# The values' product of two chunks at once over all 128 partitions, with zeros between their values

## The chip, the core and the metric

The kernel runs on one core of one Trainium2 chip. The metric is the device time of one execution in microseconds (us); less is better. Engines are named as in the profile: PE is TensorE's matmul, PEld its weight load, DVE VectorE, ACT ScalarE, POOL GpSimd, SP SyncE, which issues all transfers here.

## What is computed

Attention over local windows, then two matrix products with a gate between them. All inputs are f32.

```python
# q, k, v: [4, 8, 768, 64]; mem_k, mem_v: [4, 8, 8, 64]; w_in: [512, 2048]; w_out: [2048, 512]
for c in range(24):                                   # chunks of 32 queries
    l, r = max(0, c*32 - 16), min(768, c*32 + 32 + 8)
    k_full = concat([mem_k, k[:, :, l:r]], axis=2)    # 64 keys at most
    v_full = concat([mem_v, v[:, :, l:r]], axis=2)
    s = (1/8) * q[:, :, c*32:c*32+32] @ k_full^T
    a = exp(s - max(s)); a = a / (sum(a) + 1e-9)
    out[:, :, c*32:c*32+32] = a @ v_full
x = out as [3072 tokens, 512]
h = x @ w_in
g = where(h >= 1, h, where(h <= -1, 0, (h + 1)**2 / 4))
result = g @ w_out
```

## The kernel before, in words

The 3072 tokens are worked on in six blocks of 512 (`NB`, `TB`), each in two halves of 256 tokens, which are eight chunks of 32 queries; a chunk sees `W` = 64 keys. Eight heads are four pairs (`NP`). The two large products (`pe_hidden`, `pe_out`) run with x, gate and weights split into a rounded f32 part and a remainder (`F32R`), three terms each; the small products of the attention are plain f32 (`F32`).

The first three blocks' attention, the decoding of the weights and the first two blocks' large products are written in one hand-made order (`FIRST`, line 32; `g` is the attention of the first block in four parts, `n0` to `n3` that of the halves of the second and third block, `L` a transfer from the list `loads`, line 613, `w` and `u` a decoding). After it, a loop over (block, slice of 128 hidden columns) runs the large products of blocks three to six, and puts the attention of the next block's two halves between them (line 659): scores at slice 3 or 9 of the block, then one stage a slice: softmax, transposes, values, split. `InOrder` (line 61) keeps every engine's work in the order in which the program writes it.

A half of block three and later goes like this. `pe_scores` puts queries on the partitions of PSUM. DVE takes off the maximum, ACT the exponential, DVE divides; `transpose_prob` turns the probabilities on DVE in 32 x 32 squares, so that the 64 keys of one chunk come to lie in partitions 0 to 63 and those of another in 64 to 127 (`a` in the code counts these two). `pe_rows` (line 398) then multiplies: weights are 64 keys x 32 queries, the moving operand is 64 keys x 64 values, and the two chunks of a pair are two matmuls on the two halves of the array's rows. `rows_out` (line 416) copies the result by ACT from two PSUM banks, one for each `a`; `turn_rows` turns it on DVE, `split_high` and `split_low` make x.

`load_v` (line 133) brings the values of a half by one transfer into a tile of 8 KB a partition, a single buffer that is free once the product before has read it. The first block (`first_attention`, line 225) uses weights of 128 keys (two heads) and 64 columns, with the probabilities in a tile `pt_apart` (line 222) that GpSimd clears at the start; both the first and the second block write x^T directly. `load_first_qk` and `load_w` (lines 109 and 141) bring first q and k and the first two weight tiles in two transfers each, each of them a half of every row of its array in memory.

Of the kernel before, what the change touches and what calls it, by code (L numbers as in the profile page):

```python
# [8 lines left out]
F32 = mybir.dt.float32  # L9
F32R = mybir.dt.float32r  # L10
BF16 = mybir.dt.bfloat16
U32 = mybir.dt.uint32
# [4 lines left out]
P = 128  # L17
CHUNK, LEFT, RIGHT = 32, 16, 8
# [39 lines left out]
SLICED = (0,1)  # L58
# [13 lines left out]


@with_exitstack
def attn_ffn_kernel(ctx: ExitStack, tc: tile.TileContext, first_qk, first_v, qk, vw, w, out):
    nc = tc.nc
    engines = (nc.tensor, nc.scalar, nc.vector, nc.gpsimd, nc.sync)
    pe, act, dve, pool, sp = (InOrder(tc, e) for e in engines)
    NP = first_qk.shape[0]
    NM = 8  # L80
    D = P // 2
    W = NM + LEFT + CHUNK + RIGHT
    DM = NP * P
    NPW = w.shape[0]
    NFC = NPW
    NB = qk.shape[0] + 1
    SEQ = 24
# [1 line left out]
    n2 = 2 * DM  # L89
# [3 lines left out]
    apool = ctx.enter_context(tc.tile_pool(name="apool", bufs=1))  # L93
# [6 lines left out]
    def two_banks(tag, name):  # L100
        return ps_2.tile([P, 2, 512], F32, name=name, tag=tag)
# [3 lines left out]
    QKN = HT + HT // CHUNK * W  # L105
    VN = HT // CHUNK * W
    qk_of, v_of = {}, {}

    def load_first_qk(g, r):

        if (0, g) not in qk_of:
            if g < 2:
                t = apool.tile([P, 2, 2 * QKN], F32, name="qk0", tag="qk")
                qk_of[0, 0], qk_of[0, 1] = t[:, 0], t[:, 1]
            else:
                qk_of[0, g] = const.tile([P, 2 * QKN], F32, name=f"qk0_{g}", tag=f"w_{NPW - 5 + g}")
        at = slice(r * QKN, (r + 1) * QKN)
        sp.dma_start(qk_of[0, g][:, at], first_qk[g, :, at])

    def load_first_v(g):  # L120
        if (0, g) not in v_of:
            if g < 2:
                t = apool.tile([P, 2, 2 * VN], F32, name="v0", tag="v")
            else:
                t = const.tile([P, 2, 2 * VN], F32, name="v0_2", tag=f"w_{NPW - 1}")
            v_of[0, g - g % 2], v_of[0, g - g % 2 + 1] = t[:, 0], t[:, 1]
        sp.dma_start(v_of[0, g], first_v[g])
# [3 lines left out]
        sp.dma_start(t, qk[blk - 1, half].rearrange("p (h f) -> p h f", h=NP))  # L131

    def load_v(blk, half):
        t = v_of[blk, half] = apool.tile([P, NP, VN], F32, name="v", tag="v")
        sp.dma_start(t, vw[blk - 1, half].rearrange("p (h f) -> p h f", h=NP))


    place = {key: divmod(n, 2) for n, key in enumerate(weight_order(NFC))}
    ws, raw = {}, {}

    def load_w(i, parts=(0, 1)):
        if i not in raw:
            tag = f"w_{NPW - 6 - i}" if i < len(SLICED) else f"w_{i}"
            raw[i] = const.tile([P, 2 * n2], U32, name=f"w_{i}", tag=tag)
        a, b = parts[0] * n2, (parts[-1] + 1) * n2
        sp.dma_start(raw[i][:, a:b], w[i, :, a // 2 : b // 2].bitcast(U32))

    def weights(which, fc, part):
        i, j = place[which, fc]
# [27 lines left out]
    scores_of, prob, prob_t, banks, rows_of, turned, xts, both = {}, {}, {}, {}, {}, {}, {}, {}  # L177
    first = 2
# [40 lines left out]
    NG = 2 * 2 * 2  # L219
    PLACES = (("s", "s"), ("a0", "a0"), ("a1", "a1"), ("a1", "s"))  # L220

    pt_apart = apool.tile([P, 2, NG // 2, 2, P], F32, name="pt0", tag="pt")
    pool.memset(pt_apart, 0.0)

    def first_attention(g):
        half, u = divmod(g, 2)
        c0 = half * NCH // 2
        src = qk_of[0, g].rearrange("p (r n) -> p r n", r=2)
# [17 lines left out]
            mask(c0 + c, s[j * CHUNK : (j + 1) * CHUNK, :, :, t])  # L246
        if u == 0:
            both[half, "pr"] = apool.tile([P, 2, NG, W], F32, name="pr0", tag="pr")
        pr, pt = both[half, "pr"][:, u], pt_apart[:, u]
        n = 2 * 2  # L250
        mx = apool.tile([P, NG], F32, name="mx", bufs=2)
        m4 = mx.rearrange("p (h r t) -> p h r t", h=2, r=2)
# [143 lines left out]
            yield  # L396
        banks.pop(key)

    def pe_rows(key, outs):

        banks[key] = outs
        pt = prob_t.pop(key).rearrange("p b (h r t) q -> p b h r t q", h=2, r=NP)
        v = v_of.pop(key).rearrange("p r (t b h d) -> p r t b h d", t=2, b=2, h=2)
        for r in range(NP):
            for t in range(2):
                for b in range(2):
                    for a in range(2):
                        rows = slice(a * D, (a + 1) * D)
                        for h in range(2):
                            to, c0 = (2 * h + b) * CHUNK, (r * 2 + t) * D  # L410
                            pe.matmul(
                                outs[a][to : to + CHUNK, c0 : c0 + D],
                                pt[rows, b, h, r, t],
                                v[rows, r, t, b, h],
                                start=True,
                                stop=True,
                            )

    def rows_out(key):

        xr = rows_of[key] = apool.tile([P, NP, 2, 2, D], F32, name="xr", tag="pt")
        for a, src in enumerate(banks.pop(key)):
            act.copy(xr[:, :, :, a], src.rearrange("p (r t d) -> p r t d", r=NP, t=2))

    def x_half(x, half):
        return x[:, :, half * HT : (half + 1) * HT]
# [23 lines left out]
    def attention(key):  # L450

        pe_scores(key)
        yield
        yield from less_max(key)
        act.activation(prob[key], prob[key], AF.Exp, scale=SCALE)
        yield
        yield from normalise(prob[key])
        yield from transpose_prob(key)
        if key[0] < first:
            pe_values(key)  # L460
            yield
            x_high(key)
            yield
            yield from x_low(key)
            return
        ps = two_banks("s", "ps_x")
        pe_rows(key, [ps[:, a] for a in range(2)])
        yield
        rows_out(key)
        yield  # L470
        yield from turn_rows(key)
        split_high(key)
        yield
        yield from split_low(key)
# [131 lines left out]
    def keep_warm(n):  # L606
# [5 lines left out]

    loads = [
        (load_first_qk, 0, 0), (load_first_qk, 0, 1), (load_first_qk, 1, 0), (load_first_qk, 1, 1),
        (load_first_v, 0), (load_w, 0, (0,)), (load_w, 0, (1,)), (load_first_v, 1),
        (load_first_qk, 2, 0), (load_first_qk, 2, 1), (load_w, 1, (0,)), (load_w, 1, (1,)),
        (load_first_qk, 3, 0), (load_first_qk, 3, 1), (load_first_v, 2), (load_first_v, 3),
    ]
    loads += [(load_w, i) for i in range(2, NPW)]
# [39 lines left out]
    for s in range(first * NFC, steps):  # L659
# [3 lines left out]
            if after(k_scores)[0] < NB:  # L663
                load_qk(*after(k_scores))
        if k_values is not None:
            ps = two_banks("s", "ps_x")
            pe_rows(k_values, [ps[:, a] for a in range(2)])
            if after(k_values)[0] < NB:
                load_v(*after(k_values))
        if s > first * NFC:  # L670
# [48 lines left out]
def _lay_out(q, k, v, mem_k, mem_v, moe_w_in, moe_w_out):  # L719
# [16 lines left out]
    def transposed(a):  # L736
# [7 lines left out]
    k0 = kw.transpose(0, 4, 7, 3, 1, 2, 5, 6).reshape(NB * 2, 2 * D, NP, NCH // 2 * W)  # L744
    kw = _np.stack([kw[:, :, 0], kw[:, :, 1][..., ::-1, :, :]], axis=2)
    kw = kw.transpose(0, 4, 7, 3, 1, 2, 5, 6).reshape(NB * 2, 2 * D, NP, NCH // 2 * W)
    qk0 = _np.concatenate([qt, k0], axis=3)[0:2].reshape(2, 2 * D, 2, -1).transpose(0, 2, 1, 3)
    qk = _np.concatenate([qt, kw], axis=3).reshape(NB, 2, 2 * D, -1)[1:]
    vw = windows(mem_v, v).reshape(NB, NT, 4, NP, 2, W, D)

# [5 lines left out]
    n = DF // 128  # L756
# [3 lines left out]
        moe_w_out.reshape(n, 128, DM),  # L760
    )
    w = _np.stack([slices[which][fc] for which, fc in weight_order(n)])
    w = w.reshape(n, 2, 128, DM).transpose(0, 2, 1, 3).reshape(n, 128, 2 * DM)
    arrays = {

        "first_qk": qk0.reshape(NP, 2 * D, -1),
        "first_v": v0.reshape(NP, 2 * W, NCH * D),
        "qk": qk,
        "vw": v1.reshape(NB - 1, 2, 2 * W, -1),
        "w": _np.ascontiguousarray(w).view(_np.int64),  # L770
    }
    return {name: _np.ascontiguousarray(a) for name, a in arrays.items()}
# [23 lines left out]
```

## Time and profile before

| | |
|---|---|
| time, median of 3 runs | 591.45 us (591.18 to 591.91) |
| the profiled execution | 591.77 us, its span 590.0 us |
| granted clock of TensorE, mean | 0.999 |
| busy share of the span | PE 97%, PEld 81%, DVE 57%, ACT 44% |
| chain that ended last | PE 94%, ACT 2%, DMA 2%, DVE 1% |
| matmul records | 5364 |
| moved by DMA | 55.30 MB, 94 GB/s over the span |

The page gives, for one profiled execution, each engine's busy time, the chain of work that ended last, and groups of instructions. A line of a group reads: engine, operation, what is written <- what is read, rows * columns of the weights, partitions x columns of the moving operand, count | busy us, mean ns | idle time of the engine just before them. A plain f32 matmul leaves two records and two weight loads; one on rounded f32 leaves one. All program lines read L69, because one helper issues every operation; tiles tell the groups apart. Ends of matmuls are modelled, so spans from start to start say more than their durations.

### The profile page before, as it was taken

How to read it: one execution, taken by the hardware profiler on the slowest of the kernel's cores; microseconds unless marked ns; L12 is line 12 of the kernel's file. 1: busy time of each engine (PE TensorE's matmuls, PEld its weight loads, DVE VectorE, ACT ScalarE, POOL GpSimd, SP SyncE). 2: the span in 40 equal slices, each digit the busy share in tenths (PEclk: the TensorE clock that was granted, in tenths of full speed). 3: DMA queues.
4: the chain of work that ended last, by engine and by line, in shares of the span. 5: the costliest groups of instructions: out<-in, count | busy, mean ns of one | idle time of the engine just before them, and what ended most of it. 6: DMA issues, size and time to landing. Idle time of an engine off the chain costs nothing.

```text
span 590.0 us, 12019 instructions
## 1 busy us (share of the span) xinstructions
PE 575.1 (97%) x5364; PEld 476.4 (81%) x5364; DVE 338.0 (57%) x497; ACT 257.2 (44%) x430; POOL 2.4 (0%) x7
## 2 busy tenths in 40 slices
PE   4899999999999999999999999999999999999996
PEld 3798888888888888888888888888888888888885
DVE  4899899884545534857624765833684752322222
ACT  2997665554434324343433343333443443433331
POOL 1000000000000000000000000000000000000000
PEclk9999999999999999999999999999999999999999
DMA  8999542026000105102202222201320000200001
GB/s 309 423 418 423 216 177 71 38 92 229 5 0 12 63 0 179 43 32 108 72 1 75 106 72 109 73 1 62 117 72 2 1 1 0 73 0 1 0 1 71
DMA packets 10708, 55.30 MB, mean 94 GB/s; under 512 B 1184, under 2 KB 1184, under 8 KB 6304
## 3 DMA queue, kind: packets, MB, share of 16 engines
q1 hardware_dynamic: 10656, 54.53, 24.3%
q8 instruction: 42, 0.69, 0.5%
q14 instruction: 10, 0.08, 0.0%
HBM read 48.23 MB, written 6.29 MB: 92 GB/s over the span
## 4 chain that ended last, share of the span: by engine, by line
PE 94%; ACT 2%; DMA 2%; DVE 1%; SPq 1%; issue 0%; DVEq 0%; ACTq 0%
PE ps_h L69 45%; PE ps_o L69 44%; PE ps_x L69 3%; PE ps_s L69 2%; DMA w<-in_w_dram 2%; ACT pt L69 1%; SPq L69 1%; ACT pr L69 0%; ACT w L69 0%; ACT wr L69 0%; DVE f L69 0%; ACT gw L69 0%; ACT xth L69 0%; DVE mx L69 0%; DVE wr L69 0%
## 5 line engine op out<-in xcount | busy, mean ns | idle before, releaser
L69 PE MATMUL ps_h<-xth,wr 128*128 128x512 f32 (+1 forms) x832 | 194.7, 376 | 0.2
L69 PE MATMUL ps_o<-wr,gh 128*128 128x512 f32 x768 | 194.5, 390 | 0.0
L69 PEld LDWEIGHTS ps_h<-xth,wr 128*128 128x128 f32 x832 | 147.9, 188 | 29.7 <-DVE gw L69 0.4
L69 PEld LDWEIGHTS ps_o<-wr,gh 128*128 128x128 f32 x768 | 143.3, 188 | 29.4
L69 DVE SCALAR_TENSOR_TENSOR gw<-ps_h,gw 128x512 f32<-128x512 f32 (+1 forms) x104 | 67.3, 648 | 144.0 <-ACT gw L69 143.4
L69 ACT ACTIVATE gw<-ps_h 128x512 f32<-128x512 f32 (+1 forms) x104 | 58.5, 562 | 175.0 <-PE ps_h L69 165.9
L69 PE MATMUL ps_o<-wr,gl 128*128 128x512 f32 x384 | 106.9, 389 | 0.0
L69 PE MATMUL ps_h<-xtl,wr 128*128 128x512 f32 (+1 forms) x416 | 104.4, 373 | 0.0
L69 DVE TENSOR_TENSOR gl<-gw,gh 128x512 fp32r<-128x512 f32 (+1 forms) x104 | 67.0, 646 | 48.7 <-ACT gh L69 41.8
L69 ACT CAST gh<-gw 128x512 fp32r<-128x512 f32 (+1 forms) x104 | 60.6, 586 | 71.7 <-DVE gw L69 54.0
L69 PEld LDWEIGHTS ps_h<-xtl,wr 128*128 128x128 f32 x416 | 74.9, 188 | 13.9
L69 PEld LDWEIGHTS ps_o<-wr,gl 128*128 128x128 f32 x384 | 72.1, 188 | 15.1
L69 ACT ACTIVATE gw<-gw 128x512 f32<-128x512 f32 (+1 forms) x104 | 62.3, 599 | 3.3
L69 DVE STREAM_TRANSPOSE pt<-pr 32x512 f32<-32x512 f32 (+1 forms) x60 | 41.3, 699 | 1.2
L69 DVE STREAM_TRANSPOSE xt<-xr 32x512 f32<-32x512 f32 (+1 forms) x48 | 33.1, 700 | 11.5 <-ACT xr L69 10.8
L69 ACT ACTIVATE pr<-pr 128x1024 f32<-128x1024 f32 (+1 forms) x13 | 12.5, 962 | 35.4 <-DVE pr L69 35.3
L69 PEld LDWEIGHTS ps_s<-qk 64*32 64x32 f32 x1536 | 16.9, 112 | 11.6 <-DMA qk<-in_first_qk_dram 7.9
L69 PE MATMUL ps_s<-qk 64*32 64x64 f32 x1536 | 19.8, 240 | 6.5 <-DMA qk<-in_first_qk_dram 6.2
L69 ACT CAST wr<-f 128x1024 fp32r<-128x1024 f32 (+1 forms) x18 | 16.9, 951 | 11.1 <-DVE f L69 11.1
L69 DVE COPY ob<-ps_o 128x512 f32<-128x512 f32 (+1 forms) x16 | 9.6, 622 | 20.5 <-PE ps_o L69 20.5
L69 ACT ACTIVATE w<-w 128x1024 f32<-128x1024 f32 (+1 forms) x18 | 18.8, 1045 | 4.6 <-DMA w<-in_w_dram 4.6
L69 DVE TENSOR_TENSOR wr<-f,wr 128x1024 fp32r<-128x1024 f32 (+1 forms) x18 | 19.8, 1100 | 1.8 <-ACT wr L69 1.6
(36 smaller groups left out, 203.4 us busy)
## 6 DMA issues: line engine op xcount, KB each, us to landing
qk<-in_qk_dram SPq DMA_DIRECT2D x10, 1536.0 KB, 6.7
w<-in_w_dram SPq DMA_DIRECT2D x14, 1024.0 KB, 18.5
v<-in_vw_dram SPq DMA_DIRECT2D x10, 1024.0 KB, 4.9
out_dram<-ob SPq DMA_DIRECT2D x24, 256.0 KB, 2.1
qk<-in_first_qk_dram SPq DMA_DIRECT2D x8, 384.0 KB, 6.7
w<-in_w_dram SPq DMA_DIRECT2D x4, 512.0 KB, 10.0
v<-in_first_v_dram SPq DMA_DIRECT2D x4, 512.0 KB, 10.9
```

Of the source, the lines that this page charges most:

```text
L69: return self.tc.keep_in_program_order(getattr(self.engine, name)(*args, **kwargs))
```

## The change

From the third block on, `pe_rows` issues one matmul for both chunks of a pair: weights of 128 keys (two chunks) x 32 queries, moving 128 keys x 128 columns, in which the first chunk's values stand in partitions 0 to 63 of the first 64 columns, the second chunk's in partitions 64 to 127 of the other 64, and zeros elsewhere. So both chunks' results lie side by side in one row, and the loop over `a` is gone. For that:

- the values have one tile of 16 KB a partition, `v_apart`, with two planes (`a`). A half of block three or later comes by two transfers of 64 partitions; GpSimd clears the other 64 partitions of either plane once, before the first of them;
- the first block's and second block's values use plane 0. The cleared probabilities of the first block, one tile before, are one tile half as large and a part of plane 1;
- a result bank holds two of the four head pairs with both chunks, instead of one chunk with all pairs, and `rows_out` copies accordingly;
- first q and k and the first two weight tiles lie in memory so that each of their transfers reads one run.

```diff
+    v_apart = apool.tile([P, 2, NP * VN], F32, name="v")
...
-        sp.dma_start(qk_of[0, g][:, at], first_qk[g, :, at])
+        sp.dma_start(qk_of[0, g][:, at], first_qk[g, r])
...
     def load_v(blk, half):
-        t = v_of[blk, half] = apool.tile([P, NP, VN], F32, name="v", tag="v")
-        sp.dma_start(t, vw[blk - 1, half].rearrange("p (h f) -> p h f", h=NP))
+        src = vw[blk - 1, half]
+        if blk < first:
+            v_of[blk, half] = v_apart[:, 0].rearrange("p (r f) -> p r f", r=NP)
+            sp.dma_start(v_apart[:, 0], src)
+            return
+        v_of[blk, half] = v_apart.rearrange("p a (r f) -> p a r f", r=NP)
+        for a in range(2):
+            rows, others = (slice(x * D, (x + 1) * D) for x in (a, 1 - a))
+            if (blk, half) == (first, 0):
+                pool.memset(v_apart[others, a], 0.0)
+            sp.dma_start(v_apart[rows, a], src[rows])
...
-    def load_w(i, parts=(0, 1)):
+    def load_w(i, part=None):
...
-        a, b = parts[0] * n2, (parts[-1] + 1) * n2
-        sp.dma_start(raw[i][:, a:b], w[i, :, a // 2 : b // 2].bitcast(U32))
+        if part is None:
+            sp.dma_start(raw[i], w[i - len(SLICED)].bitcast(U32))
+        else:
+            sp.dma_start(raw[i][:, part * n2 : (part + 1) * n2], first_w[i, part].bitcast(U32))
...
-    pt_apart = apool.tile([P, 2, NG // 2, 2, P], F32, name="pt0", tag="pt")
-    pool.memset(pt_apart, 0.0)
+    pt_apart = [
+        apool.tile([P, NG // 2, 2, P], F32, name="pt0", tag="pt"),
+        v_apart[:, 1, 0 : NG * P].rearrange("p (n t q) -> p n t q", t=2, q=P),
+    ]
+    for pt in pt_apart:
+        pool.memset(pt, 0.0)
...
-    def pe_rows(key, outs):
-
-        banks[key] = outs
+    def pe_rows(key):
+
+        ps = banks[key] = two_banks("s", "ps_x")
+        o = ps.rearrange("p b (r t a d) -> p (b r) t a d", r=NP // 2, t=2, a=2)
         pt = prob_t.pop(key).rearrange("p b (h r t) q -> p b h r t q", h=2, r=NP)
-        v = v_of.pop(key).rearrange("p r (t b h d) -> p r t b h d", t=2, b=2, h=2)
+        v = v_of.pop(key).rearrange("p a r (t b h d) -> p a r t b h d", t=2, b=2, h=2)
         for r in range(NP):
             for t in range(2):
                 for b in range(2):
-                    for a in range(2):
-                        rows = slice(a * D, (a + 1) * D)
-                        for h in range(2):
-                            to, c0 = (2 * h + b) * CHUNK, (r * 2 + t) * D
-                            pe.matmul(
-                                outs[a][to : to + CHUNK, c0 : c0 + D],
-                                pt[rows, b, h, r, t],
-                                v[rows, r, t, b, h],
-                                start=True,
-                                stop=True,
-                            )
+                    for h in range(2):
+                        to = (2 * h + b) * CHUNK
+                        pe.matmul(
+                            o[to : to + CHUNK, r, t], pt[:, b, h, r, t], v[:, :, r, t, b, h], start=True, stop=True
+                        )
 
     def rows_out(key):
 
         xr = rows_of[key] = apool.tile([P, NP, 2, 2, D], F32, name="xr", tag="pt")
-        for a, src in enumerate(banks.pop(key)):
-            act.copy(xr[:, :, :, a], src.rearrange("p (r t d) -> p r t d", r=NP, t=2))
+        ps = banks.pop(key)
+        for b in range(2):
+            r = slice(b * NP // 2, (b + 1) * NP // 2)
+            act.copy(xr[:, r], ps[:, b].rearrange("p (r t a d) -> p r t a d", r=NP // 2, t=2, a=2))
```

On PE the order of the products is otherwise as it was. This is the place of the second half of block three, still in the hand-made order, before the change (`ps_x` is the result, `v` the values, `pt` the transposed probabilities, `ps_h` and `ps_o` the two large products):

```order
168 L69 MATMUL ps_o<-wr_1129,gl 128x512 x4
169 L69 MATMUL ps_h<-xth,wr_1132 128x512 x8
170 L69 MATMUL ps_h<-xtl,wr_1132 128x512 x4
171 L69 MATMUL ps_x<-v,pt 32x64 x64
172 L69 MATMUL ps_h<-xth,wr_924 128x512 x8
173 L69 MATMUL ps_h<-xtl,wr_924 128x512 x4
```

And the same place after it:

```order
169 L69 MATMUL ps_o<-wr_1128,gl 128x512 x4
170 L69 MATMUL ps_h<-xth,wr_1131 128x512 x8
171 L69 MATMUL ps_h<-xtl,wr_1131 128x512 x4
172 L69 MATMUL ps_x<-v,pt 32x128 x32
173 L69 MATMUL ps_h<-xth,wr_924 128x512 x8
174 L69 MATMUL ps_h<-xtl,wr_924 128x512 x4
```

64 matmuls of 32 x 64 results are 32 of 32 x 128; their neighbours stay.

On SP's queue, the values of block three and the four transfers of the first block's result behind them, before:

```order
32 L69 DMA qk<-in_qk_dram 128x3072 [waits DMAHW3_49,DMAHW2_49,PE_49]
33 L69 DMA v<-in_vw_dram 128x2048 [waits DMAHW1_49,PE_49]
34 L69 DMA out_dram<-ob 128x512 [waits DMAHW5_49,DVE_49]
35 L69 DMA out_dram<-ob 128x512 [waits Activation_49]
36 L69 DMA out_dram<-ob 128x512 [waits DMAHW7_49,DVE_49]
```

And after:

```order
32 L69 DMA qk<-in_qk_dram 128x3072 [waits DMAHW3_49,DMAHW2_49,PE_49]
33 L69 DMA v<-in_vw_dram 64x2048 [waits DMAHW1_49,PE_49]
34 L69 DMA v<-in_vw_dram 64x2048 [waits DMAHW5_49,Pool_49]
35 L69 DMA out_dram<-ob 128x512 [waits DVE_49]
36 L69 DMA out_dram<-ob 128x512 [waits DMAHW7_49,Activation_49]
```

The second piece waits for GpSimd, and the transfers of results stand behind it. On POOL the clearing is two rows more, at the end of its work:

```order
11 L69 MEMSET v 64x2048 [waits DMAHW1_49,DMAHW3_49,PE_49,Pool_49]
12 L69 MEMSET v 64x2048 [waits Activation_49]
```

The first of them waits for PE, which reads block two's values, and for the transfers that brought them.

## Rows read from the trace of the kernel before

**Rows 1.** The page's chain of work that ended last, shares of the span by engine and by written tile, and the busy time of each engine.

```profile
PE 575.1 (97%) x5364; PEld 476.4 (81%) x5364; DVE 338.0 (57%) x497; ACT 257.2 (44%) x430; POOL 2.4 (0%) x7
...
PE 94%; ACT 2%; DMA 2%; DVE 1%; SPq 1%; issue 0%; DVEq 0%; ACTq 0%
PE ps_h L69 45%; PE ps_o L69 44%; PE ps_x L69 3%; PE ps_s L69 2%; DMA w<-in_w_dram 2%; ACT pt L69 1%; SPq L69 1%; ACT pr L69 0%; ACT w L69 0%; ACT wr L69 0%; DVE f L69 0%; ACT gw L69 0%; ACT xth L69 0%; DVE mx L69 0%; DVE wr L69 0%
```

**Rows 2.** The timeline of PE around the first values' product of block three (133 us) and the last product of this kind (469.5 us), and the group of records running in 470.8 to 471.1 us: start us, length us, engine, operation, count.

```profile
133.48 1.49 PE L69 MATMUL ps_x<-v,pt 64*32 64x64 f32 x128
134.89 0.50 PE L69 MATMUL ps_o<-wr,gh 128*128 128x512 f32 x1
...
469.55 1.49 PE L69 MATMUL ps_x<-v,pt 64*32 64x64 f32 x128
470.97 2.11 PE L69 MATMUL ps_h<-xth,wr 128*128 128x512 f32 x8
...
470.58 0.46 PE L69 MATMUL ps_x<-v,pt 64*32 64x64 f32 x24
```

**Rows 3.** The view of the tile ps_x: count, then the duration of a record in ns (least, median, greatest), first and last start in us.

```profile
L69 PE MATMUL ps_x<-v,pt x1024: 212/216/240, 133.5 to 470.8; 64*32 64x64 f32 x171
```

**Rows 4.** The timeline of PE in 469.4 to 469.8 us: the records of the product that start in this stretch.

```profile
469.55 0.46 PE L69 MATMUL ps_x<-v,pt 64*32 64x64 f32 x32
```

**Rows 5.** The timeline of PE: two products of the first block (128 rows, 64 weight columns, 64 moving columns, 16 matmuls each), and one of the second block (64 rows, 64 weight columns, 32 moving columns, 64 matmuls).

```profile
27.27 1.15 PE L69 MATMUL ps_x<-pt,v 128*64 128x64 f32 x32
28.60 1.15 PE L69 MATMUL ps_x<-pt,v 128*64 128x64 f32 x32 [0.18 <-ACT pt L69]
...
117.35 2.07 PE L69 MATMUL ps_x<-pt,v 64*64 64x32 f32 x128
```

**Rows 6.** PE's groups by shape, the first large product's remainder term at 256 and at 512 moving columns (rounded f32; | busy us, mean ns).

```profile
L69 PE MATMUL ps_h<-xtl,wr 128*128 128x512 f32 x352 | 94.1, 389 | 0.0
...
L69 PE MATMUL ps_h<-xtl,wr 128*128 128x256 f32 x64 | 10.3, 283 | 0.0
```

**Rows 7.** Durations of a record in ns (least, median, greatest): the first block's product in 28.65 to 29.55 us, and the transposes with the identity.

```profile
L69 PE MATMUL ps_x<-pt,v x32: 222/222/270, 28.6 to 29.5; 128*64 128x64 f32 x32
...
L69 PE MATMUL ps_h<-ident,pr x16: 272/417/476, 13.3 to 27.1; 128*128 128x128 f32 x16
```

**Rows 8.** The timeline around the last of these products on DVE and ACT: the transposes of the probabilities ahead of it, the copies of its result (two of 0.59 us, merged), the turning and the cast to x.

```profile
464.91 4.23 DVE L69 STREAM_TRANSPOSE pt<-pr 128x512 f32<-128x512 f32 x6
471.08 1.07 ACT L69 COPY xr<-ps_x 128x512 f32<-128x512 f32 x2 [0.55 <-PE ps_x L69]
472.18 4.19 DVE L69 STREAM_TRANSPOSE xt<-xr 128x512 f32<-128x512 f32 x6 [0.94 <-ACT xr L69]
476.41 1.05 ACT L69 CAST xth<-xt 128x1024 fp32r<-128x1024 f32 x1 [1.12 <-DVE xt L69]
...
L69 ACT COPY xr<-ps_x x16: 587/590/594, 135.0 to 471.6; 128x512 f32<-128x512 f32 x16
```

**Rows 9.** The page's DMA issues of values (KB each, median us from issue to landing), GpSimd's memset at the start, and SP's queue from 119 to 132 us.

```profile
v<-in_vw_dram SPq DMA_DIRECT2D x10, 1024.0 KB, 4.9
...
0.73 1.80 POOL L69 MEMSET pt<- 128x2048 f32 x1 [0.29 <-POOLq L782]
...
119.48 0.33 SPq L69 DMA_DIRECT2D v<-in_vw_dram  x1
131.15 5.78 SPq L69 DMA_DIRECT2D out_dram<-ob  x4
```

**Rows 10.** The start-up: the piece of the chain that ends with the first weights' landing and the decoding behind it; SP's issue of the strided weight halves; who TensorE waited for in 0 to 34 us (total, times, longest); and busy times by stretch, whose last three columns are PEclk, DMA share and GB/s.

```profile
4.01 10.14 DMA w<-in_w_dram
14.17 0.68 ACT w L69
...
9.84 2.33 SPq L69 DMA_DIRECT2D w<-in_w_dram  x3
...
PE ps_s L69 <- DMA qk<-in_first_qk_dram: 6.2, 4, 2.9
...
2.00:6.00 4.00, 2.44 (x67) 1.03 (x65) 0.25 (x2) 0.02 (x1) 0.97 (x3) 1.00 0.92 318
6.00:10.00 4.00, 1.18 (x64) 0.94 (x64) 2.40 (x7) 0.79 (x2) 0.00 (x0) 1.00 0.97 322
10.00:14.00 4.00, 1.88 (x68) 1.67 (x69) 3.73 (x10) 1.13 (x2) 0.00 (x0) 1.00 1.03 413
14.00:18.00 4.00, 2.72 (x34) 2.35 (x34) 2.39 (x5) 3.51 (x16) 0.00 (x0) 1.00 1.04 426
```

More of the change, by code (lines that the diff above doesn't have):

```diff
@@ L74, in attn_ffn_kernel @@
 @with_exitstack
-def attn_ffn_kernel(ctx: ExitStack, tc: tile.TileContext, first_qk, first_v, qk, vw, w, out):
+def attn_ffn_kernel(ctx: ExitStack, tc: tile.TileContext, first_qk, first_v, qk, vw, first_w, w, out):
     nc = tc.nc
@@ L83, in attn_ffn_kernel @@
     DM = NP * P
-    NPW = w.shape[0]
+    NPW = len(SLICED) + w.shape[0]
     NFC = NPW
@@ L122, in load_first_v @@
             if g < 2:
-                t = apool.tile([P, 2, 2 * VN], F32, name="v0", tag="v")
+                t = v_apart[:, 0].rearrange("p (g n) -> p g n", g=2)
             else:
@@ L248, in first_attention @@
             both[half, "pr"] = apool.tile([P, 2, NG, W], F32, name="pr0", tag="pr")
-        pr, pt = both[half, "pr"][:, u], pt_apart[:, u]
+        pr, pt = both[half, "pr"][:, u], pt_apart[u]
         n = 2 * 2
@@ L465, in attention @@
             return
-        ps = two_banks("s", "ps_x")
-        pe_rows(key, [ps[:, a] for a in range(2)])
+        pe_rows(key)
         yield
@@ L614, in attn_ffn_kernel @@
         (load_first_qk, 0, 0), (load_first_qk, 0, 1), (load_first_qk, 1, 0), (load_first_qk, 1, 1),
-        (load_first_v, 0), (load_w, 0, (0,)), (load_w, 0, (1,)), (load_first_v, 1),
-        (load_first_qk, 2, 0), (load_first_qk, 2, 1), (load_w, 1, (0,)), (load_w, 1, (1,)),
+        (load_first_v, 0), (load_w, 0, 0), (load_w, 0, 1), (load_first_v, 1),
+        (load_first_qk, 2, 0), (load_first_qk, 2, 1), (load_w, 1, 0), (load_w, 1, 1),
         (load_first_qk, 3, 0), (load_first_qk, 3, 1), (load_first_v, 2), (load_first_v, 3),
@@ L665, in attn_ffn_kernel @@
         if k_values is not None:
-            ps = two_banks("s", "ps_x")
-            pe_rows(k_values, [ps[:, a] for a in range(2)])
+            pe_rows(k_values)
             if after(k_values)[0] < NB:
@@ L746, in _lay_out @@
     kw = kw.transpose(0, 4, 7, 3, 1, 2, 5, 6).reshape(NB * 2, 2 * D, NP, NCH // 2 * W)
-    qk0 = _np.concatenate([qt, k0], axis=3)[0:2].reshape(2, 2 * D, 2, -1).transpose(0, 2, 1, 3)
+    qk0 = _np.concatenate([qt, k0], axis=3)[0:2].reshape(2, 2 * D, 2, 2, -1).transpose(0, 2, 3, 1, 4)
     qk = _np.concatenate([qt, kw], axis=3).reshape(NB, 2, 2 * D, -1)[1:]
@@ L762, in _lay_out @@
     w = _np.stack([slices[which][fc] for which, fc in weight_order(n)])
-    w = w.reshape(n, 2, 128, DM).transpose(0, 2, 1, 3).reshape(n, 128, 2 * DM)
+    w = w.reshape(n, 2, 128, DM)
+    first_w = _np.ascontiguousarray(w[: len(SLICED)])
+    w = w[len(SLICED) :].transpose(0, 2, 1, 3).reshape(-1, 128, 2 * DM)
     arrays = {
-        "first_qk": qk0.reshape(NP, 2 * D, -1),
+        "first_qk": qk0.reshape(NP, 2, 2 * D, -1),
         "first_v": v0.reshape(NP, 2 * W, NCH * D),
@@ L769, in _lay_out @@
         "vw": v1.reshape(NB - 1, 2, 2 * W, -1),
+        "first_w": first_w.view(_np.int64),
         "w": _np.ascontiguousarray(w).view(_np.int64),
```

## The prediction

> **What bounds the kernel now.** I read four views, from the whole to the single product. First the chain that ended last: 94% of the span lies on TensorE, and only about 5% on ACT, DMA and DVE together [rows 1]; DVE is busy 57% and ACT 44% of the span. So from the end of the start-up on, a microsecond taken from TensorE's row of work shortens the kernel and one added to it lengthens it. The reader should see next what the edited product is in that chain: one values' product of a half block stands there with 1.42 us, from its first matmul to the next product's first [rows 2]. There are eight of them (blocks three to six, two halves; 1024 records, two for each of 8 x 64 matmuls) [rows 3]. They hold 8 x 1.42 = 11.4 us. All of them gone would be 1.9% of the time, so the change moves single microseconds. A measurement of this kernel can tell about 0.2%, 1.2 us, from no change.
>
> Then the product itself. Now it is 64 matmuls with 64 rows of contraction, 32 columns of weights and 64 moving columns, spread over two row halves and four column groups of the array. In the first 0.24 us of it (0.46 us less one record's 0.22) 16 matmuls start, 15 ns each [rows 4]; over the whole it is (1.49 - 0.22) / 64 = 20 ns each [rows 2]. So the array took them faster than TensorE went on being fed. That is what makes halving the number of instructions look good.
>
> **What the change puts there.** 32 matmuls of 128 rows, 32 weight columns and 128 moving columns. Half of the rows meet zeros: the useful products are the same, the array positions times columns are doubled (32 x 128 x 128 against 64 x 64 x 64). Only the four column groups are left to work side by side. Three prices decide.
>
> *Instructions.* 32 at 20 ns are 0.64 us. No bound any more.
>
> *Weight loads.* The nearest row is the product of the second block: 64 x 64 weights, 32 moving columns, (2.07 - 0.22) / 64 = 29 ns each, with two row halves loading at once, so 58 ns for 64 columns in one row half [rows 5]. The first block's product has 128 rows and 64 weight columns and goes at (1.15 - 0.22) / 16 = 58 ns too [rows 5]. A load of 32 columns over all rows is then 29 ns, and 32 of them 0.93 us.
>
> *Streams.* This is the disputed price. A matmul on rounded f32 leaves one record: 389 ns at 512 columns, 283 ns at 256 [rows 6], which is 0.41 ns per column, one cycle at 2.4 GHz (the clock granted is 1.00 of that in every stretch of [rows 10]), and 177 ns that don't depend on columns. A plain f32 product leaves two records. With the same 177 ns taken off, its record costs (216 - 177) / 64 = 0.61 ns per column in the edited product [rows 3], (222 - 177) / 64 = 0.70 in the first block's [rows 7] and, for the transposes with the identity, (272 - 177) / 128 = 0.74 [rows 7]. Two of the three lie nearer to two cycles (0.83) than to one; the 177 ns are from the full array, and if a narrower piece needs less, the columns cost more. I take two cycles for each of the two records. Then 128 columns occupy their column group for 128 x 2 x 0.83 = 213 ns, four groups side by side let one matmul through every 53 ns, and 32 take 1.71 us. The first block's product says how well the places overlap: 64 columns would be 107 ns alone, two column groups 53, and the row has 58, so each round loses some 5 ns. Eight rounds of 218 ns are 1.74 us. The hand-over to the next product is in the 1.42 us as the last start at 470.82 to the next product's 470.97 [rows 2], 0.15 us less the stream of about 0.04; with 0.11 us added, the new product takes 1.85 us. The loads (29 ns each) lie beside the streams.
>
> The Trainium skill, FP8 and Floating Point Precision, section TensorE Precision Notes, says that a true FP32 product makes four passes through the array. By it the 32 matmuls take 1.71 us; by the durations as they stand (0.61 to 0.74 ns) they take 1.25 to 1.52 us, and the product 1.36 to 1.63 us.
>
> So each product goes from 1.42 to 1.85 us, +0.43, and eight of them +3.4 us, all on the path. Bounds: 1.07 us each where only loads count (0.93 + 0.11 + one load ahead), and 3.7 us where the column groups take turns (116 ns for 128 columns, from the first block's 58 for 64).
>
> **The other edits.** *Copies of the result.* ACT copies two banks of 128 x 512 at 0.59 us as before [rows 8]; the first can start at half of the product. DVE turns the rows for 4.2 us, the split follows at 476.4, and x is wanted three steps (some 16 us) later: nothing. The transposed probabilities are ready at 469.14, 0.41 us ahead of their product [rows 8]; the longer products push that further ahead: nothing.
>
> *Values loaded in two pieces.* Each 64 partitions; the whole took 4.9 us in the median [rows 9], and the buffer is free for tens of us before its next use. Nothing, even at twice the price.
>
> *Zeros.* Before the first values of block three GpSimd clears two pieces of 64 x 2048, once PE has read block two's values at 119.5. The memset of 128 x 2048 took 1.80 us [rows 9]; two of these at most 3.6 us, so the second piece is issued by 123.1 and lands by 128.0, against its use at 133.48 [rows 2]. SP's next transfer waits until 131.15 anyway [rows 9], so nothing stands behind that wait. 5.5 us of cover; each us beyond would cost one.
>
> *First loads laid out in one run.* Start-up hangs on transfers: from 4.01 to 14.17 the chain is the second half of the first weights, and TensorE waits 6.2 us for first q and k [rows 10]. From 2 to 10 us they moved at 318 to 322 GB/s, later at 413 to 426 [rows 10]. But from 10 to 14 us transfers with the same strides went at 413, so striding is not what is slow: gain at least 0, at most (1 - 320/420) x 8 = 1.9 us. I take 0.4, nearer to nothing for that reason.
>
> **Sum.** The profiled execution took 591.77 us (its span 590.0), 0.32 above the median of 591.45. +3.4 - 0.4 = +3.0 gives 594.8 for it and **594.5 us** for the median.
>
> **Rivals.** *(a) The streams hide behind the loads; faster.* If a column costs a record 0.45 ns or less (about one cycle), four column groups take 128 x 2 x 0.45 / 4 = 29 ns and the loads set the pace: 1.07 us each, -0.35 x 8 = -2.8, with the start-up 588.2 us. For it: loads alone explain all three products (58, 29 and 58/4 = 14.5 against 15 ns), and the edited product's own 0.61 lies as near to one cycle as to two. Against: the other two durations, and the tail would have to be longer on fewer columns. 0.17.
>
> *(b) In between; no change.* Streams at 0.61 ns as measured: 1.25 + 0.11 = 1.36 us each, -0.5 us in all, with the start-up 590.5; or the forecast's streams with a start-up that gains all of 1.9 and rounds without loss. 0.08.
>
> *(c) The column groups take turns.* Nothing here shows four groups over all 128 rows at work together. 3.7 us each, +2.3 x 8 = +18.2: 609 us. Against: with two cycles the first block's 58 ns needs two groups at once, and the edited product's 15 ns all eight places. 0.03. The Trainium skill, TensorE: Matmul & The Clock Gate, Part 3, says that a weight load overlaps matmuls in flight only where the row group differs, which here it never does; the first block's 58 ns for a product with 53 ns of loads speaks against that. The same part gives 2.38 times for three column groups; four at that efficiency would make 2.16 us of the 1.71 and some 598 us in all.
>
> *(d) It is not carried out as told.* The built order has 32 matmuls of 32 x 128 where 64 stood, so only the counts of records could surprise: below 0.01.
>
> **Numbers.** Forecast 0.72, (a) 0.17, (b) 0.08, (c) 0.03. The forecast's own range is 592.7 (rounds lose nothing, start-up gains all) to 597 (rounds lose 30 ns more each, start-up nothing). With (b) taken in, 590.3 to 597.0 leaves out (a) and (c), 2 in 10. Faster by over 0.2%: (a), with a little of (b), 0.18. Within: 0.07. Slower: 0.75.
>
> **What would show it.** Right: the eight products at 1.75 to 1.95 us from start to next start, 512 records, eight rounds about 216 to 220 ns apart, and no wait ahead of the product at block three. The streams' price is wrong if rounds stand 110 to 120 ns apart (a), 150 to 190 (b). The start-up term is wrong if the first decode starts over 0.9 us earlier than 14.17, or later than it. A wait of TensorE for values or zeros near 133 us would refute the cover of 5.5 us.

## The result and the profile after

| | before | after |
|---|---|---|
| time, median of six runs | 591.4 us (590.98 to 591.91) | 595.56 us (595.21 to 596.02) |
| ratio, 95% interval | | 1.0067 [1.0057, 1.0077] |
| profiled execution, its span | 591.77, 590.0 us | 596.02, 594.2 us |
| one values' product, first start to the next product's first (mean of eight) | 1.415 us | 1.884 us |
| first start of the first such product (block three) | 133.48 us | 133.96 us |

The changed kernel is 4.2 us slower. The page of the kernel after (its span, the busy time of each engine, the chain by engine and by tile) shows the same bound as [rows 1]: TensorE's row of work.

```profile
span 594.2 us, 11015 instructions
PE 578.3 (97%) x4852; PEld 478.3 (80%) x4852; DVE 337.9 (57%) x497; ACT 257.2 (43%) x430; POOL 6.1 (1%) x10
PE 94%; ACT 2%; DVE 1%; DMA 1%; issue 0%; SPq 0%; DVEq 0%; ACTq 0%
PE ps_h L69 44%; PE ps_o L69 44%; PE ps_x L69 3%; PE ps_s L69 2%; DMA qk<-in_first_qk_dram 1%; ACT pr L69 1%; ACT wr L69 0%; ACT v L69 0%; ACT pt L69 0%; ACT w L69 0%; DVE den L69 0%; DVE f L69 0%; SPq L69 0%; ACT xth L69 0%; ACT gw L69 0%
```

TensorE has 512 records fewer than in [rows 1] (5364 to 4852) and is busy 3.2 us more (575.1 to 578.3). In the chain the transfer named is now the first q and k instead of the first weights; that returns below.

The products themselves, where [rows 2] had 1.42 us from 469.55 to 470.97: the timeline of PE after the change at block three and at the last product, then its first 0.12 us, and the records' durations in the view of the tile ps_x (count, least, median and greatest ns).

```profile
133.39 0.64 PE L69 MATMUL ps_h<-xtl,wr 128*128 128x256 f32 x4
133.96 1.96 PE L69 MATMUL ps_x<-v,pt 128*32 128x128 f32 x64
135.85 0.98 PE L69 MATMUL ps_o<-wr,gh 128*128 128x512 f32 x3
...
473.33 1.95 PE L69 MATMUL ps_x<-v,pt 128*32 128x128 f32 x64
475.22 0.96 PE L69 MATMUL ps_h<-xth,wr 128*128 128x512 f32 x3
...
473.33 0.32 PE L69 MATMUL ps_x<-v,pt 128*32 128x128 f32 x4
...
L69 PE MATMUL ps_x<-v,pt x512: 272/273/297, 134.0 to 475.0; 128*32 128x128 f32 x171
```

Each product is 1.89 us from its start to its neighbour's (135.85 - 133.96, 475.22 - 473.33), and no wait stands ahead of it. Its 64 records start in bursts of four, 109.2 ns apart (the second burst 133 ns behind the first). A matmul leaves two records, so two bursts hold one round of four matmuls (one for each column group); a round takes 218 ns, and eight rounds 1.75 us. In the row for the first 0.12 us one whole burst of four stands and the second has not begun. Eight products hold (1.884 - 1.415) x 8 = **3.75 us** more. The first began 0.48 us later in this execution; together that is 4.23, and the spans differ by 4.2. Nothing else on the path changed length in this execution. The 0.48 us are no fixed part of the change: when the same kernel was run again, that product began at 133.48. Where such half microseconds come from is read behind the last experiment.

The cover of the other edits, where [rows 8, 9] answer: POOL's zeros, SP's queue (two spaces stand ahead of a count there), the page's issues of values, and DVE and ACT behind the last product.

```profile
120.07 3.67 POOL L69 MEMSET v<- 64x2048 f32 x2 [116.99 <-PE ps_x L69]
...
119.93 1.18 SPq L69 DMA_DIRECT2D v<-in_vw_dram  x2
131.61 6.29 SPq L69 DMA_DIRECT2D out_dram<-ob  x4
...
v<-in_vw_dram SPq DMA_DIRECT2D x16, 512.0 KB, 5.9
...
476.46 4.19 DVE L69 STREAM_TRANSPOSE xt<-xr 128x512 f32<-128x512 f32 x6 [1.47 <-ACT xr L69]
480.68 1.05 ACT L69 CAST xth<-xt 128x1024 fp32r<-128x1024 f32 x1 [1.15 <-DVE xt L69]
```

The two memsets take 3.67 us, the values land some 6 us after issue instead of 4.9, and the first product of 133.96 still waits for neither. SP was done issuing both pieces of the values at 119.93 + 1.18 = 121.11, before the memsets ended at 120.07 + 3.67 = 123.74, so the second piece did not wait for them, though the forecast counted on that wait.

### The profile page after: what moved, and what is told of

It is laid out like the page before. It is cut to its first block, busy times and chain, and to the rows that moved or that the text cites. A ratio compares the mean times of both kernels' runs of the same rounds, so it can differ in the third digit from the quotient of the medians.

```text
span 594.2 us, 11015 instructions
## 1 busy us (share of the span) xinstructions
PE 578.3 (97%) x4852; PEld 478.3 (80%) x4852; DVE 337.9 (57%) x497; ACT 257.2 (43%) x430; POOL 6.1 (1%) x10
## 4 chain that ended last, share of the span: by engine, by line
PE 94%; ACT 2%; DVE 1%; DMA 1%; issue 0%; SPq 0%; DVEq 0%; ACTq 0%
PE ps_h L69 44%; PE ps_o L69 44%; PE ps_x L69 3%; PE ps_s L69 2%; DMA qk<-in_first_qk_dram 1%; ACT pr L69 1%; ACT wr L69 0%; ACT v L69 0%; ACT pt L69 0%; ACT w L69 0%; DVE den L69 0%; DVE f L69 0%; SPq L69 0%; ACT xth L69 0%; ACT gw L69 0%
## 5 line engine op out<-in xcount | busy, mean ns | idle before, releaser
L69 PE MATMUL ps_s<-qk 64*32 64x64 f32 x1536 | 19.7, 239 | 6.9 <-DMA qk<-in_first_qk_dram 6.4
```

The lines of the kernel that those rows point to most:

```text
L69: return self.tc.keep_in_program_order(getattr(self.engine, name)(*args, **kwargs))
```

## The experiments

**The theory** is the forecast's: a plain f32 matmul occupies its column group for two records of two cycles a column, the four groups work side by side, and doubling the moving columns therefore doubles the product's time in the array. **Its rivals:** the streams are cheap and the weight loads or the number of instructions set the pace; the four groups over all 128 rows don't fully work at once; the product costs nothing and the new loads or zeros do.

### What a matmul costs by its columns, rows and places

In the changed kernel each of the eight products is followed by 32 more matmuls on the same data. Their places and sizes differ from product to product; a pair (b, h) in the list stands for column group 2h + b of the array.

```
+        again(key, o, pt, v)
...
+    AGAIN = {
+        (2, 0): ([(0, 0)] * 4, "both"),
+        (2, 1): ([(0, 0), (0, 1)] * 2, "both"),
+        (3, 0): ([(0, 0), (1, 0)] * 2, "both"),
+        (3, 1): ([(0, 0), (1, 0), (0, 1), (1, 1)], "both"),
+        (4, 0): ([(0, 0), (0, 1), (1, 0), (1, 1)], "one"),
+        (4, 1): ([(0, 0)] * 4, "one"),
+        (5, 0): ([(0, 0)] * 4, "half"),
+        (5, 1): ([(0, 0), (0, 1), (1, 0), (1, 1)], "half"),
+    }
```

The body of `again` is left out. "both" is 128 moving columns, "one" 64 of them, "half" 64 of them with 64 rows.

> The changed kernel with 32 more matmuls behind each of the eight values' products, which write the same values again: another choice of places in each half. The result stays whole; only the rates of the added matmuls are read, in ns from start to start. Theory A (two cycles per column and record, all four column groups at work at once): 128 moving columns in one column group 213 to 220 ns, in two groups 107 to 112 whichever two, in four 54 to 56 in either order; 64 moving columns over all rows in one group 107 to 112, in four groups 27 to 30; 64 rows and 64 columns in one place 107 to 112, in four groups of one row half 27 to 30. Rival B (one cycle per column and record, only two column groups at once): one group 107 to 112, two groups 54 to 56, four groups 54 to 56; 64 columns in one group 54 to 59, in four 27 to 30; 64 rows in one place 54 to 59. Rival C (a weight load waits for the streams in flight): no difference between one group and four. The whole is longer by the added work, 8 x 1 to 7 us, which tells nothing.

Measured: 620.01 us, in a single run. In the windows of PE (start and end, length, busy us and the records that run in the stretch, PEclk, DMA share, GB/s) one stretch lies inside the added part of each product, in the order of the table above:

```profile
135.00:141.00 6.00, 6.00 (x61) 1.00 0.13 46
197.60:200.60 3.00, 3.00 (x62) 1.00 0.03 5
259.30:262.30 3.00, 3.00 (x62) 1.00 0.02 5
299.20:300.60 1.40, 1.40 (x64) 1.00 0.06 12
359.10:359.70 0.60, 0.60 (x60) 1.00 0.00 0
396.40:399.40 3.00, 3.00 (x61) 1.00 0.03 5
458.20:461.20 3.00, 3.00 (x56) 1.00 0.02 5
498.40:499.00 0.60, 0.60 (x58) 1.00 0.10 27
```

The counts take in records begun before the stretch, so the spacing of the starts was taken from the records one by one; the rows show the proportions. Per matmul of two records:

| added matmuls | one column group | two | four |
|---|---|---|---|
| 128 rows, 128 columns | 218 ns | 109 and 109 | 54.6 |
| 128 rows, 64 columns | 112 | | 28 |
| 64 rows, 64 columns | 112 | | 28 |

Three things are read from it. The price is 218 ns for 128 columns and 112 for 64: two records of 109 ns, and 109 / 128 = 0.85 ns a column and record, which is 2% above two cycles (0.83 ns) at the granted 2.4 GHz (PEclk 1.00 in every stretch). The groups divide it exactly, two by two and four by four, whichever two are taken. And rows cost nothing: 64 rows in one place take as long as 128. The kernel before uses the two row halves for different products at once [rows 4]; with zeros in one of them that half is spent. Both rivals on the product fall: with the same loads, 32 weight columns over 128 rows, the matmuls of 64 columns went through at 28 ns, half of 54.6, so the loads are no bound of the changed product; and the groups don't take turns.

The Trainium skill, FP8 and Floating Point Precision, section TensorE Precision Notes, gives four passes for a true FP32 product; 218 ns for 128 columns are about four cycles a column (213 ns), so these runs agree. The Trainium skill, TensorE: Matmul & The Clock Gate, Part 3, lets a weight load overlap matmuls in flight only where the row group differs; here every matmul over 128 rows has the same row group and new weights, and four groups still went 218 / 54.6 = 4.0 times as fast as one. On this form of matmul the measurement speaks against that rule, and against taking its 2.38 times for three groups as a ratio for four.

### The loads alone and the product alone

The loads alone: the kernel before, with the first q, k and weights laid out in one run each.

```
-        sp.dma_start(qk_of[0, g][:, at], first_qk[g, :, at])
+        sp.dma_start(qk_of[0, g][:, at], first_qk[g, r])
...
-        a, b = parts[0] * n2, (parts[-1] + 1) * n2
-        sp.dma_start(raw[i][:, a:b], w[i, :, a // 2 : b // 2].bitcast(U32))
...
+            sp.dma_start(raw[i][:, part * n2 : (part + 1) * n2], first_w[i, part].bitcast(U32))
```

> The kernel before with one part of the change alone: first q and k and the first two weight tiles read in one run per transfer. It tells where the start-up's half microsecond comes from (the first values' product of block three starts 0.48 us later in the changed kernel). If it comes from the order in which these transfers land: +0.3 to +0.6 us, ratio 1.0005 to 1.0010, and that product starts near 133.9 us. If from the tile that first probabilities and values share: 0 us, the product at 133.5 us. The forecast's term was -0.4 us (ratio 0.9993, 133.1 us).

The product alone: the changed kernel with these lines set back.

```
-        sp.dma_start(qk_of[0, g][:, at], first_qk[g, r])
+        sp.dma_start(qk_of[0, g][:, at], first_qk[g, :, at])
...
-            sp.dma_start(raw[i][:, part * n2 : (part + 1) * n2], first_w[i, part].bitcast(U32))
+        a, b = (0, 2 * n2) if part is None else (part * n2, (part + 1) * n2)
+        sp.dma_start(raw[i][:, a:b], w[i, :, a // 2 : b // 2].bitcast(U32))
```

> The changed kernel with its first loads laid out and read as before. The products alone are 8 x 0.469 = 3.75 us. If the start-up's half microsecond comes from the first loads: +3.7 us, ratio 1.0063, the first values' product of block three at 133.5 us. If it comes from the shared tile: +4.2 us, ratio 1.0071, the product at 133.9 us.

And the changed kernel itself on the same chip, unedited:

> The changed kernel as it is, on the same chip as the two others, for the difference between them. +4.2 us, ratio 1.0071, the first values' product of block three at 133.9 us, if the start-up repeats from run to run; if it scatters, it lies anywhere between 133.4 and 134.0 us and the ratio between 1.0060 and 1.0072.

Measured against the kernel before on the same chip (591.5 us):

| | time | ratio |
|---|---|---|
| loads alone | 591.69 us | 1.0004 [0.9995, 1.0013] |
| product alone | 595.34 us | 1.0065 [1.0051, 1.0079] |
| whole change | 595.30 us | 1.0066 [1.0053, 1.0078] |

The product alone is the whole change, +3.8 us, as eight times 0.47 says (3.75). The loads are worth nothing that can be told: by the interval between 0.3 us gained and 0.8 us lost. The reason lies in the start-up. Here are first the kernel after (PE's and ACT's timelines, PE's waits in 0 to 34 us, the chain, and the windows as in [rows 10]), then the product alone, whose loads are strided as before, and last the second scores (those of the first block's second part, `g` = 1) of the kernel before.

```profile
8.75 1.19 PE L69 MATMUL ps_s<-qk 64*32 64x64 f32 x64 [2.99 <-DMA qk<-in_first_qk_dram]
13.26 0.67 ACT L69 ACTIVATE w<-w 128x512 f32<-128x512 f32 x1 [1.02 <-DMA w<-in_first_w_dram]
...
PE ps_s L69 <- DMA qk<-in_first_qk_dram: 6.4, 4, 3.0
...
2.11 6.59 DMA qk<-in_first_qk_dram
8.75 1.20 PE ps_s L69 x62
...
2.00:6.00 4.00, 2.44 (x67) 1.03 (x65) 0.10 (x1) 0.02 (x1) 1.01 (x3) 1.00 0.91 299
6.00:10.00 4.00, 1.19 (x64) 0.94 (x64) 1.62 (x5) 0.63 (x1) 0.00 (x0) 1.00 1.02 388
10.00:14.00 4.00, 1.18 (x64) 0.94 (x64) 3.89 (x11) 1.96 (x3) 0.00 (x0) 1.00 1.03 413
```

```profile
7.00 1.18 PE L69 MATMUL ps_s<-qk 64*32 64x64 f32 x64 [1.36 <-DMA qk<-in_first_qk_dram]
14.23 0.65 ACT L69 ACTIVATE w<-w 128x512 f32<-128x512 f32 x1 [3.70 <-DMA w<-in_w_dram]
...
2.00:6.00 4.00, 2.45 (x67) 1.03 (x65) 0.18 (x2) 0.02 (x1) 1.02 (x3) 1.00 0.93 353
6.00:10.00 4.00, 1.18 (x64) 0.95 (x64) 3.20 (x8) 1.28 (x3) 0.00 (x0) 1.00 0.98 297
```

```profile
7.74 1.18 PE L69 MATMUL ps_s<-qk 64*32 64x64 f32 x64 [2.16 <-DMA qk<-in_first_qk_dram]
```

Laid out in one run, the transfers move faster from 6 to 10 us (388 against 297 GB/s here, 322 in [rows 10]), but slower from 2 to 6 us (299 against 353, 318 in [rows 10]). Over both stretches that is 344 against 325 and 320 GB/s, so less is gained than the second stretch alone lets one think. The weights' second half is decoded 0.9 us earlier (13.26 against 14.23, 14.17 before). But the second q and k come later: their scores start at 8.75 instead of 7.00, and 7.74 before. The chain no longer passes the weights' transfer; it passes the q and k that were held up. The first product of block three starts anywhere from 133.1 to 134.1 us, with no side to either layout. What decides it is read below, with one run more.

### The feeding of small matmuls

In the kernel before, four of the products are followed by 64 more matmuls of its own form, with moving columns halved, weight columns halved, or both.

```
+        again(key, outs, pt, v)
...
+    AGAIN = {(2, 0): (CHUNK, D), (2, 1): (CHUNK, D // 2), (3, 0): (CHUNK // 2, D // 2), (3, 1): (CHUNK // 2, D)}
...
+                            pe.matmul(
+                                outs[a][to : to + wide, c0 : c0 + cols],
+                                pt[rows, b, h, r, t, 0:wide],
+                                v[rows, r, t, b, h, 0:cols],
```

> The kernel before, with 64 more matmuls behind four of its values' products, which write some of the same values again; the result stays whole. First half of block three: the same 64 once more. Second: with 32 moving columns instead of 64. First half of block four: 32 columns and 16 weight columns instead of 32. Second: 64 columns and 16 weight columns. Theory F (after the first 16, TensorE is fed no faster than 20 ns a matmul, whatever its size): all four 19 to 22 ns a matmul. Rival W (weight loads set the pace): 19 to 22 in the first two, half of that with 16 weight columns. Rival S (streams set the pace): 19 to 22 with 64 columns, half of that with 32. If F holds, halving the instructions could have paid up to 1.42 - 0.9 us a product, had the array's work not doubled.

Measured: 608.41 us, in a single run. The product's own 64 start as in [rows 4], the first 16 at 15 to 17 ns, the rest at 20.25 ns. The added ones come at 20.0 ns (64 columns, 32 weights), 17.9 (32 columns), 17.3 (both halved) and 19.7 (64 columns, 16 weights). Halving the columns should have taken the array's 13 to 14 ns to 7; it took 2 ns off. Both rivals fall, as no form comes near half of 20 ns; the theory's 19 to 22 ns for every size held for the two forms with 64 columns and missed for the two with 32. So in most of its product the kernel before was bound by something that goes by the number of matmuls and hardly by their size. I call it feeding; what it is in the engine, these runs don't show. What I had not expected is the stop in the timeline of PE:

```profile
133.17 2.17 PE L69 MATMUL ps_x<-v,pt 64*32 64x64 f32 x201
137.24 0.78 PE L69 MATMUL ps_x<-v,pt 64*32 64x64 f32 x55 [1.90 <-issue]
...
193.18 2.21 PE L69 MATMUL ps_x<-v,pt 64*32 64x64 f32 x216
197.81 0.55 PE L69 MATMUL ps_x<-v,pt 64*32 64x32 f32 x40 [2.42 <-issue]
...
254.55 2.31 PE L69 MATMUL ps_x<-v,pt 64*32 64x64 f32 x231
259.26 0.31 PE L69 MATMUL ps_x<-v,pt 64*16 64x32 f32 x25 [2.40 <-issue]
...
PE ps_x L69 <- issue: 8.6, 4, 2.4
```

Each run of 128 such matmuls stood still once, for 1.9 to 2.4 us, after 201 to 231 records (100 to 115 matmuls), and no semaphore ended it. The rates above are those ahead of the stop. Right behind it the smallest matmuls came at 10.3 ns each (the 25 records from 259.26 on), against 17.3 ahead of it: the array and the weight loads take them faster than they are fed. As for the stop itself, the next instructions not being at hand would fit. The page counts 46 transfers of instructions in this run against 42 before, and the transfers one by one show one of 16 KB beside every stop: they begin at 134.90, 195.46, 256.79 and 295.92 us, take 0.9 to 1.0 us, and TensorE goes on 1.3 to 1.6 us after each has ended. No run moved these transfers, so that they cause the stop is not shown.

### Half of the streams

In the changed kernel the product streams one of the two chunks, and the copy out writes it in place of both.

```
-                            o[to : to + CHUNK, r, t], pt[:, b, h, r, t], v[:, :, r, t, b, h], start=True, stop=True
+                            o[to : to + CHUNK, r, t, 0], pt[:, b, h, r, t], v[:, 0, r, t, b, h], start=True, stop=True
...
+        for a in range(2):
+            act.copy(to[:, :, a], src[:, :, 0])
```

> The changed kernel with 64 moving columns instead of 128: only the first of the two chunks of a pair is computed, and its values are copied in the place of the second's. As many instructions, weight loads and rows as in the changed kernel, half of its streams. Theory A with the feed of 17 to 20 ns: four matmuls a 112 ns, 32 in 0.90 us, the product 1.05 to 1.12 us, 8 x -0.33 = -2.6 us against before, ratio 0.9955. If something else than streams made the changed product long (its 128 rows, its loads, the change of tile shape), it stays near 1.88 us and the ratio near 1.0065.

Measured: 588.49 us against 591.14 of the kernel before, 0.9957 [0.9944, 0.9971]. The timeline of PE at the last product:

```profile
466.62 1.10 PE L69 MATMUL ps_x<-v,pt 128*32 128x64 f32 x64
467.65 1.65 PE L69 MATMUL ps_h<-xth,wr 128*128 128x512 f32 x6
```

With the same 32 instructions, their weight loads, the zeros and the transfers, the product takes 1.03 us instead of 1.88. That is the saving the halved instructions would have brought had the columns not doubled: below the 1.42 us of before. So the doubled columns, and nothing else in the change, make it slower.

### First q and k ahead of the weights

Since the one-run layout only exchanged the late weights for late q and k, the last run puts the other order to it: loads alone, with L5, the transfer of the first half of the first weights, issued behind L9, one more transfer of q and k.

```
-    L0 L1 L3 g0 L2 g0 g0 L5 g1 g0 L9 g0 g0 u0 g1 g1 g1 g0 L8 L6 u0 g0 g1 L12 g0 g1 L4 g1 g2 g0 g1 g0
+    L0 L1 L3 g0 L2 g0 g0 g1 g0 L9 L5 g0 g0 u0 g1 g1 g1 g0 L8 L6 u0 g0 g1 L12 g0 g1 L4 g1 g2 g0 g1 g0
```

> The kernel before with its first loads in one run each, and the first half of the first weights issued one place later, behind one more transfer of q and k. In the runs so far the contiguous reads bring the first weights' second half 0.8 to 1.7 us earlier, but the second transfer of q and k later, and the chain of the start-up moves from the weights to q and k. If that exchange ate the gain: the second scores start before 8.0 us, the first values' product of block three at 132.6 to 133.2 us, -0.3 to -0.9 us against before, ratio 0.9985 to 0.9995. If the start-up is bound by the bytes in front of the first large products, whatever their order: 133.1 to 134.1 us, ratio 0.9995 to 1.0010.

Measured: 591.86 us against 591.6, 1.0004 [0.9995, 1.0013]. PE's and ACT's timelines:

```profile
8.02 1.19 PE L69 MATMUL ps_s<-qk 64*32 64x64 f32 x64 [2.35 <-DMA qk<-in_first_qk_dram]
13.64 0.68 ACT L69 ACTIVATE w<-w 128x512 f32<-128x512 f32 x1 [2.14 <-DMA w<-in_first_w_dram]
```

The scores start 0.9 us earlier than with loads alone (8.02 against 8.90) and the weights are 0.2 us later (13.64 against 13.40). The time does not move; in this execution (591.53 us) the first product of block three starts at 133.24 us, which is the second of the two outcomes expected. None of the versions that compute everything beats the kernel before.

What decides that start shows when all nine executions are set side by side, by the timelines of PE and ACT (us):

| | first loads | second scores | second half of weights decoded | first product of block three |
|---|---|---|---|---|
| before | strided | 7.74 | 14.17 | 133.48 |
| product alone | strided | 7.00 | 14.23 | 133.51 |
| 64 small matmuls added | strided | 7.73 | 13.86 | 133.17 |
| after | one run | 8.75 | 13.26 | 133.96 |
| after, again | one run | 8.27 | 12.71 | 133.48 |
| loads alone | one run | 8.90 | 13.40 | 134.12 |
| 32 matmuls added | one run | 7.88 | 13.66 | 133.11 |
| half of the streams | one run | 8.06 | 12.52 | 133.36 |
| q and k ahead | one run | 8.02 | 13.64 | 133.24 |

In the three strided ones the product starts 119.3 us after the decoding, in the six others 125.2 to 125.3 us after the second scores. In all nine it is the later of the two sums, to within 0.1 us. So two chains run side by side through the start-up. In the kernel before the one through q and k ends only 0.5 us behind the other (7.74 + 125.2 = 132.9 against 133.48): by this rule faster weights alone could not have gained more than that, and with the loads in one run the second scores came 0.1 to 1.2 us later than before, which ate the gain. The rule is read off these executions; the run with q and k ahead is the only one that changed the order.

## Why the prediction was right, and where it was off

**The bound.** Right: every microsecond added to TensorE's row appeared in the time (+3.75 in the products, +3.8 in the product alone).

**The streams' price, the disputed step.** Right. It was taken as two cycles a column and record against durations that gave less; the runs measured 0.85 ns between starts in one place. The record's duration of the changed product, less the forecast's fixed part, still says (273 - 177) / 128 = 0.75. But with half of the columns the same piece of the array leaves records of 219 ns, so (273 - 219) / 64 = 0.84 ns a column, and the fixed part is some 165 ns: the 177 ns of the full array are too large for a narrower piece, as the forecast allowed. The spacing of starts has no fixed part to take off. The 53 ns a matmul and 218 ns a round of the forecast came out at 54.6 and 218. One reading behind it was wrong without harm: PEclk stands at 1.00 in every stretch of [rows 10], but the transposes with the identity, whose least duration the forecast took, last 417 to 476 ns up to 22.3 us and 272 or 273 from 26.8 us on, so in the start-up the records look like the lower clock. The rows that the price rests on lie behind it.

**Loads and instructions.** Right that neither is the bound: at 64 columns the same 32 matmuls went through at 28 ns each. The forecast's 29 ns for a load of 32 columns is thus no more than an upper end; the 58 ns of the first block's products [rows 5], read there as loads or as streams, fit the streams (64 columns, two groups: 112 / 2 = 56). The 53 ns of loads that the forecast's rival (c) sets against these 58 are shown by no run; 53 ns is what it had worked out for the streams.

**The hand-over.** 0.11 us was mis-sized: 1.884 us less eight rounds of 218 ns leaves 0.14. Eight times 0.03 is 0.24 us of the 3.75.

**The copies, the two pieces of the values, the zeros.** Right, at nothing. The zeros took 3.67 us against at most 3.6; the values' landing took 5.9 us against 4.9. The cover was counted from an issue at 123.1 behind the zeros; in fact the second piece was issued by 121.11, so there was more cover than the 5.5 us, and no wait appears at 133.96. ACT and DVE only wait longer for the product (ACT for ps_x 8.4 us in all, 4.2 before).

**The start-up.** Wrong: -0.4 us was taken, and none was there. Its own test, a decode over 0.9 us earlier than 14.17, was met at the edge (13.26) and by 1.5 us when the kernel was run again (12.71), so the weights did come earlier; the step that failed is the one from landing to end. The chain of [rows 10] named the weights, and I took what the weights gain as gained. A second chain, through the second q and k, lay 0.5 us behind; it became the longer one, and the same change had made it later.

**The sum.** 594.5 forecast, 595.56 measured: 0.35 us in the products (3.75 against 3.4), 0.4 in the start-up, the rest within the scatter between measurements (595.30 for the same kernel in the next one). Both misses have the same sign, so no error hid another.

**The rivals.** That the loads set the pace (a) needed rounds 110 to 120 ns apart, and the in-between (b) 150 to 190: they are 218. The column groups taking turns (c) needed 116 ns a matmul: it is 54.6. That the product is not built as told (d) fell to 512 records.

**What stays open.** The form with rounded f32, which leaves one record a matmul, was not tried. What feeding is, and what stops the dense runs of small matmuls, is not shown. Nor do these runs explain the second block's 29 ns a matmul [rows 5]: by the streams' price (estimated from the 0.85 ns, 32 columns in four places) it would take 14 ns, and small matmuls were fed at 17 to 20.

## What to carry to other kernels

Packing two small products into one instruction by setting zeros between saves an instruction and spends the array: count places of the array times columns first, and the instructions only where the array leaves time over. Here the array time of the kernel before lay hidden under the feeding (64 matmuls at 13 to 15 ns of array, 20 ns of feeding), and doubled it came out on top (32 at 54.6 ns). Take the price of a column from the spacing of starts in one place, and where a transfer on the chain gets faster, ask which transfer pays for it and how far behind the next chain ends.

## What was not expected of the hardware

Dense matmuls of 64 rows, 16 or 32 weight columns and 32 or 64 moving columns went on being fed at 17 to 20 ns, and after 100 to 115 of them TensorE stood still for 1.9 to 2.4 us with no semaphore that the trace names, each time beside one transfer of instructions. Transfers laid out in one run moved at 376 to 397 GB/s from 6 to 10 us, strided ones at 297 to 322; over 2 to 10 us it was 337 to 352 against 318 to 325, and the time was the same.
